# Row groups of four, reshuffles into 32 partitions, and a filter load over both halves in a fused FFT and MLP kernel

## The chip, the cores and the metric

The kernel runs on one core of one Trainium2 chip. The metric is device time in microseconds (us), smaller is better. Of the 25 runs of the kernel before that stood beside the three batches of experiments, 21 lie within 0.3% of their batch's median (357.52 to 362.08 us in all); a difference is called real here when it is over 2%, or when a 95% interval of the ratio excludes 1.

An engine name stands for the hardware unit in the profile: PE is TensorE, DVE is VectorE, ACT is ScalarE, POOL is GpSimd, and SP is SyncE, which here only issues transfers. "Hole" means a time in which TensorE had nothing in it. The granted clock is the share of its full speed at which TensorE was allowed to run.

## The reference

The kernel computes a forward pass and all its gradients (outputs 0 to 7). The part that matters here is the first block: a LayerNorm, a two-dimensional real FFT, a product with a learned complex filter, and the inverse FFT.

```python
def _A_ref(x, w_r, w_i):                      # x: 1 x 2048 x 448, w_r and w_i: 2048 x 225, bf16
    X = rfft2(x.astype(float32), axes=(-2, -1))
    W = w_r + 1j * w_i
    return irfft2(X * W, s=(S, D), axes=(-2, -1)).astype(bfloat16)

h  = x + _A_ref(layernorm(x), A_w_r, A_w_i)
h2 = h + _B_ref(layernorm(h), w1, b1, w2, b2)  # two-layer MLP with GELU over the sequence axis
# outputs: h2, then the gradients of x, w_r, w_i, w1, b1, w2, b2 for a given grad_out
```

## The kernel before

The FFT over 2048 rows is done as matmuls in two stages. In the first ("rows"), `row_a` transforms one of 16 row blocks and `row_b` transforms along the columns. The result has 128 partitions in one order; the second stage (`s2_stage`) wants 16 groups of 128 partitions in another. A DMA from SBUF to SBUF, called **reshuffle** below, puts it there. The tile `D2` is written by eight reshuffles of 226 KB in each direction:

```python
def row_b(h, quarters=False):
    u, c = divmod(h, 2)                       # a group is two rows
    ...                                       # four matmuls, then a cast into cs
    if c:
        defer(RESH_LAG, lambda: nc.sync.dma_start(out=D2[u:u + 121:8]..., in_=cs...), cs)
```

`D2[u:u + 121:8]` is 16 partitions at a stride of eight, over all 16 groups. While a reshuffle is under way, TensorE is kept busy with matmuls that do not depend on it ("fillers": `fill(20)` ahead of the forward second stage, `fill(N_FILL_B[2])` with 40 ahead of the backward one). Those that are not used up remain for the end of the kernel.

The filter, 2048 x 225 values of two bytes for each of its real and imaginary parts (921.6 KB a part), is loaded into `W_rows` and later copied by ScalarE and VectorE into a padded layout. The order of the partitions must match that of `D2`:

```python
def w_load():
    for c_, d in ((0, A_w_r), (1, A_w_i)):
        for p0, p1, j0, j1, row, dims in ((0, 64, 0, 16, 0, [[16 * DF, 4]]), (64, 112, 0, 16, 97, [[-16 * DF, 3]]),
                                          (112, 128, 0, 15, 113, []), (112, 128, 15, 16, 64, [])):
            nc.sync.dma_start(out=W_rows[p0:p1, c_, j0:j1, :],
                              in_=bass.AP(d.tensor, d.offset + row * DF,
                                          [[P * DF, 16]] + dims + [[1, (j1 - j0) * DF]]))
            yield
```

The list in square brackets is the access pattern of the source, slowest dimension first: `[stride, count]`. In every load of the kernel before, the slowest dimension of the source has a count of **16**. The loads of the real part are issued in the row loop at rows 9 to 12, those of the imaginary part at the start of the second stage, between two transposed blocks of w2 for the fillers (`"TWWWWTTT"`: T is a block of w2, W a filter load). All go through the queue of SyncE.

## Time and profile before

The kernel before takes 358.42 us (median of 3 runs, 358.37 to 358.54); its profiled run has a span of 357.2 us and a mean granted clock of 0.987. TensorE is busy in 341.5 us of it, so all that can be gained without removing matmuls is 15.7 us of holes. The table is made from the stage table that the prediction shows (a stretch less TensorE's busy time in it):

| Stretch | Holes, us | What ends the largest |
|---|---|---|
| start and forward rows, 0 to 31 | 6.86 | first loads; cast of a row on ScalarE, 1.61 |
| end of rows, 31 to 50.3 | 0.04 | |
| forward second stage, 50.3 to 105 | 2.94 | block of w2 from the DMA queue, 1.50; filter copies on ScalarE, 0.95 |
| middle, 105 to 236 | 0.15 | |
| backward rows, 236 to 254.5 | 0.70 | last LayerNorm rows on VectorE |
| backward second stage and inverse, 254.5 to 345 | 0 | |
| end, from 345 | 4.99 | cast, store and landing after the last matmul |

Two views of the transfers will be compared with the kernel after. The first is the table by stretches of four microseconds: start and end of the stretch, its length, busy time and count of PE, weight loads, DVE, ACT and POOL, then the granted clock, the share of the 16 DMA engines that was busy, and GB/s.

```profile
39.00:43.00 4.00, 3.96 (x37) 2.75 (x35) 3.20 (x8) 3.66 (x9) 0.00 (x0) 1.00 1.02 173
```

At 39 to 43 us the loads of the real filter part and the reshuffles run. The second view is the chain of waits, where one DMA stands in the whole second stage (start, duration, what):

```profile
52.00 8.60 DMA rO<-in_B_w_dram
```

That is the w2 block behind the imaginary filter part.

### The profile page before, as it was taken

How to read it: one execution, taken by the hardware profiler on the slowest of the kernel's cores; microseconds unless marked ns; L12 is line 12 of the kernel's file. 1: busy time of each engine (PE TensorE's matmuls, PEld its weight loads, DVE VectorE, ACT ScalarE, POOL GpSimd, SP SyncE). 2: the span in 40 equal slices, each digit the busy share in tenths (PEclk: the TensorE clock that was granted, in tenths of full speed). 3: DMA queues.
4: the chain of work that ended last, by engine and by line, in shares of the span. 5: the costliest groups of instructions: out<-in, count | busy, mean ns of one | idle time of the engine just before them, and what ended most of it. 6: DMA issues, size and time to landing. Idle time of an engine off the chain costs nothing.

```text
span 357.2 us, 6450 instructions
## 1 busy us (share of the span) xinstructions
PE 341.5 (96%) x2133; PEld 183.8 (51%) x2133; DVE 252.5 (71%) x679; ACT 213.8 (60%) x457; POOL 67.7 (19%) x227
## 2 busy tenths in 40 slices
PE   6898998899999999999999999999999999999994
PEld 2455665555645555555555555544444444455641
DVE  5897626992884888775226978784498766499994
ACT  4669836965986545504221355565477776588883
POOL 8667000000220000001001111110000000056771
PEclk9699999999999999999999999999999999999998
DMA  8999999847999999997886999999976878999996
GB/s 207 287 200 234 200 198 162 169 140 252 280 292 336 302 348 241 252 246 218 194 192 134 192 210 194 221 175 264 264 214 201 238 196 236 245 215 221 247 286 234
DMA packets 147672, 81.62 MB, mean 229 GB/s; under 512 B 95480, under 2 KB 139768, under 8 KB 147384
## 3 DMA queue, kind: packets, MB, share of 16 engines
q1 hardware_dynamic: 147352, 80.83, 94.7%
q8 instruction: 16, 0.26, 0.3%
q10 hardware_dynamic: 288, 0.39, 0.3%
q14 instruction: 16, 0.13, 0.1%
HBM read 27.56 MB, written 23.89 MB: 144 GB/s over the span
## 4 chain that ended last, share of the span: by engine, by line
PE 79%; ACT 7%; DVE 6%; DMA 4%; issue 2%; SPq 1%; POOL 0%; ACTq 0%; DVEq 0%
PE ps_mm L218 66%; PE ps_ff L218 13%; DMA rO<-in_B_w_dram 2%; ACT rO L82 2%; DVE stats L82 2%; ACT rG L82 1%; DMA rA<-in_A_x_dram 1%; DVE r L82 1%; ACT Ut L82 1%; DVE rA L82 1%; DVE rS L82 1%; SPq L297 1%; ACT Vt L82 1%; ACT rX L82 0%; ACT rS L82 0%
## 5 line engine op out<-in xcount | busy, mean ns | idle before, releaser
L218 PEld LDWEIGHTS <-r 128*128 128x128 bf16 (+2 forms) x660 | 61.7, 104 | 49.6 <-issue 2.7
L218 PEld LDWEIGHTS <-rS 128*128 128x128 bf16 (+2 forms) x496 | 40.5, 99 | 38.3 <-issue 7.0
L218 PE MATMUL ps_mm<-rD,r 128*128 128x448 bf16 x224 | 44.5, 352 | 0.0
L82 ACT CAST rO<-ps_mm 128x512 bf16<-128x512 f32 (+1 forms) x62 | 33.5, 583 | 13.8 <-PE ps_mm L218 11.1
L218 PE MATMUL ps_mm<-rC,rE 128*128 128x448 bf16 x144 | 36.0, 369 | 3.3 <-DMA rC<-in_grad_out_dram 3.3
L218 PEld LDWEIGHTS <-rst 128*128 128x128 bf16 (+1 forms) x320 | 23.8, 97 | 29.3 <-issue 13.5
L82 ACT CAST r<-ps_ff 128x452 bf16<-128x452 f32 x58 | 33.4, 576 | 8.8 <-PE ps_ff L218 8.4
L218 PE MATMUL ps_mm<-r,rst 128*128 128x512 bf16 (+3 forms) x192 | 36.4, 353 | 0.0
L218 PE MATMUL ps_mm<-rB,r 128*128 128x448 bf16 x160 | 31.2, 352 | 0.1
L218 PE MATMUL ps_mm<-rG,rst 128*128 128x512 bf16 (+1 forms) x128 | 28.2, 380 | 0.0
L82 ACT ACTIVATE r<-ps_mm,rstd_h 128x448 bf16<-128x448 f32 x16 | 10.1, 633 | 26.1 <-PE ps_mm L218 26.1
L82 ACT ACTIVATE r<-rC 128x448 bf16<-128x448 bf16 x16 | 9.1, 572 | 26.8 <-DMA out_dram<-r 12.9
L82 DVE SCALAR_TENSOR_TENSOR r<-ps_mm,b2col,r 128x448 bf16<-128x448 f32 x16 | 10.9, 682 | 19.9 <-PE ps_mm L218 17.9
L82 DVE CAST rO<-ps_mm 128x512 bf16<-128x512 f32 (+1 forms) x18 | 11.8, 658 | 15.2 <-PE ps_mm L218 14.3
L82 ACT ACTIVATE rG<-rG 128x896 bf16<-128x896 bf16 x14 | 13.3, 950 | 14.9 <-DVE rG L82 14.6
L218 PEld LDWEIGHTS <-rO 128*128 128x128 bf16 (+1 forms) x165 | 15.6, 98 | 12.2 <-DMA rO<-in_B_w_dram 1.8
L218 PE MATMUL ps_mm<-rE,rS 128*128 128x448 bf16 x112 | 21.5, 352 | 0.0
L82 ACT CAST rG<-ps_mm 128x512 bf16<-128x512 f32 (+1 forms) x33 | 16.6, 541 | 7.3 <-PE ps_mm L218 7.2
L1180 POOL TENSOR_SCALAR lcol<-lcol 128x1 f32<-128x1 f32 x16 | 8.5, 530 | 65.1 <-ACT r L82 65.1
L218 PE MATMUL ps_mm<-rC,rO 128*128 128x448 bf16 x80 | 19.1, 352 | 1.5 <-DMA rO<-in_B_w_dram 1.5
L1371 POOL TENSOR_SCALAR lcol<-lcol 128x1 f32<-128x1 f32 x16 | 5.5, 342 | 78.5 <-ACT r L82 78.5
L218 PEld LDWEIGHTS <-rE 128*128 128x128 bf16 x148 | 14.4, 101 | 11.3 <-issue 5.0
(198 smaller groups left out, 662.6 us busy)
## 6 DMA issues: line engine op xcount, KB each, us to landing
out_dram<-rO SPq DMA_DIRECT2D x34, 256.0 KB
r<-in_B_w_dram SPq DMA_DIRECT2D x5, 1024.0 KB
r<-r SPq DMA_DIRECT2D x16, 226.0 KB
r<-r SPq DMA_DIRECT2D x32, 113.0 KB
rS<-in_B_w_dram SPq DMA_DIRECT2D x4, 896.0 KB
out_dram<-rG SPq DMA_DIRECT2D x10, 256.0 KB
rO<-in_B_w_dram SPq DMA_DIRECT2D x2, 1024.0 KB
w_d<-rG SPq DMA_DIRECT2D x1, 1808.0 KB
```

The lines of the kernel that those rows point to most:

```text
L82: fn(**kw)
L218: nc.tensor.matmul(out, lhsT=lhsT, rhs=rhs, start=start, stop=stop)
L297: nc.sync.dma_start_transpose(out=wT, in_=B_w2[j * P:(j + 1) * P, :].rearrange("f (t c) -> f t c", c=P))
L1180: gp_.tensor_scalar(out=m1, in0=ms, scalar1=-1.0 / D, scalar2=None, op0=ALU.mult)
L1371: gp_.tensor_scalar(out=m1, in0=ms, scalar1=-2.0 / D, scalar2=None, op0=ALU.mult)
```

## The change

The intent: a group is four rows, so that a reshuffle covers 32 partitions at a stride of four and half of the second-stage groups, and the second stage's first groups need only the first halves. Each filter load then fills 32 partitions, every fourth over both halves of SBUF. As the transforms are grouped differently, they start later, the store of the filter gradient has 12 pieces, and fewer fillers stand ahead of the second stages. The core of the diff follows. The rest relabels generated constants to the new order, cuts the buffers for row groups from three to two (of twice the size) and those for folded rows from four to three, and adapts the backward rows and the store:

```diff
-N_FILL_B = (16, 16, 40, 8, 24, 8)
+N_FILL_B = (16, 16, 30, 8, 24, 8)
...
-            for p0, p1, j0, j1, row, dims in ((0, 64, 0, 16, 0, [[16 * DF, 4]]), (64, 112, 0, 16, 97, [[-16 * DF, 3]]),
-                                              (112, 128, 0, 15, 113, []), (112, 128, 15, 16, 64, [])):
-                nc.sync.dma_start(out=W_rows[p0:p1, c_, j0:j1, :],
+            for b, j0, j1, row, up in ((0, 0, 15, 0, 113), (0, 15, 16, 15, 49), (1, 0, 16, 16, 81), (2, 0, 16, 32, 49), (3, 0, 16, 48, 17)):
+                nc.sync.dma_start(out=W_rows[b:P:4, c_, j0:j1, :],
                                   in_=bass.AP(d.tensor, d.offset + row * DF,
-                                              [[P * DF, 16]] + dims + [[1, (j1 - j0) * DF]]))
+                                              [[up * DF, 2], [P * DF, 16], [1, (j1 - j0) * DF]]))
...
-            defer(RESH_LAG, lambda: nc.sync.dma_start(out=D2[u:u + 121:8].rearrange("p g c k -> p (g c k)"),
+            defer(RESH_LAG, lambda: nc.sync.dma_start(out=D2[u:u + 125:4, 8 * e:8 * e + 8].rearrange("p g c k -> p (g c k)"),
...
-        row_b(t - 1)
+        row_b(t - 3)
         if t == NT - 1:
-            row_b(t)
+            for i in range(t - 2, NT):
+                row_b(i)
...
-        for _ in range((9, 10, 11, 12).count(t)):
+        for _ in range((9, 9, 10, 11, 12).count(t)):
             next(w_loads)
...
-    fill(20)
+    fill(14)
...
-            for kind in "TWWWWTTT":
+            for kind in "TWWWWWTTT":
...
-    GW_AT = (1, 3, 5, 6, 7, 9, 11, 12)
+    GW_AT = (1, 2, 3, 4, 5, 6, 7, 8, 9, 10, 11, 12)
```

More of the change, by code (lines that the diff above doesn't have):

```diff
@@ L356 @@
     fr = ftmp(448, 64)
-    gp_.iota(fr.rearrange("p (c i g) -> p c i g", c=2, i=4), pattern=[[1, 2], [16, 4], [2, 8]], base=0,
+    gp_.iota(fr.rearrange("p (c q i g) -> p c q i g", c=2, q=2, i=4), pattern=[[1, 2], [8, 2], [16, 4], [2, 4]], base=0,
              channel_multiplier=0, allow_small_or_imprecise_dtypes=True)
@@ L432, in gen_R @@
         t = ftmp(2688, P).bitcast(I32)
-        tv = t.rearrange("p (c h x) -> p c h x", c=2, h=2)
-        f2 = fr.rearrange("p (c x) -> p c x", c=2)
+        tv = t.rearrange("p (c h x) -> p c h x", c=4, h=2)
+        f2 = fr.rearrange("p (c x) -> p c x", c=4)
         for h in range(2):
@@ L443, in decode @@
         a4, fc, s_, c_, f_ = col(), col(), col(), col(), col()
-        floor_div(eng, a4, pcolb, 64)
-        gp_madd(s_, a4, -64.0, pcolb)
-        floor_div(eng, fc, s_, 8)
-        gp_madd(s_, fc, -8.0, s_)
-        gp_madd(s_, s_, 2.0, a4)
+        floor_div(eng, a4, pcolb, 32)
+        gp_madd(s_, a4, -32.0, pcolb)
+        floor_div(eng, fc, s_, 4)
+        gp_madd(s_, fc, -4.0, s_)
+        gp_madd(s_, s_, 4.0, a4)
         floor_div(eng, c_, fc, 4)
@@ L501, in gen_UV @@
             d0 = dst[:, :, 0:64].rearrange("p g (l f) -> p g l f", f=4)
-            d1 = dst[:, :, 64:112].rearrange("p g (l f) -> p g l f", f=3)
+            d1 = dst[:, :, 64:P].rearrange("p g (l f) -> p g l f", f=4)
             for j in range(4):
                 m = msk[:, j:j + 1]
-                dj = d1[:, :, :, j - 1] if j else dst[:, :, 112:128]
-                for o, c in ((d0[:, :, :, j], 0), (dj, 1)):
+                for o, c in ((d0[:, :, :, j], 0), (d1[:, :, :, j], 1)):
                     if load[1] + 0.24 < load[0] + 0.38:
@@ L564, in w_io @@
         for c_, d in ((0, dr), (1, di)):
-            for p0, p1, g0, g1, row, dims in ((0, 64, 0, 16, 0, [[16 * DF, 4], [1, 16 * DF]]),
-                                              (64, 112, 0, 16, 112, [[-DF, 48], [1, DF]]),
-                                              (112, 128, 1, 16, 127, [[-DF, 15], [1, DF]]),
-                                              (112, 128, 0, 1, 64, [[1, DF]])):
-                sb = Wv[p0:p1, g0:g1, c_, 0:DF]
+            for sl, g0, g1, row, dims in ((slice(0, 64), 0, 16, 0, [[16 * DF, 4], [1, 16 * DF]]),
+                                          (slice(65, P, 4), 0, 16, 112, [[-DF, 16], [1, DF]]),
+                                          (slice(66, P, 4), 0, 16, 96, [[-DF, 16], [1, DF]]),
+                                          (slice(67, P, 4), 0, 16, 80, [[-DF, 16], [1, DF]]),
+                                          (slice(64, P, 4), 1, 16, 127, [[-DF, 15], [1, DF]]),
+                                          (slice(64, P, 4), 0, 1, 64, [[1, DF]])):
+                sb = Wv[sl, g0:g1, c_, 0:DF]
                 d_ap = bass.AP(d.tensor, d.offset + row * DF, [[P * DF, 16]] + dims)
@@ L615, in rowbase @@
         return 32 * (s_ // 4) + s_ % 4
-    blk_ring = ring(rS, 0, 3, 8, 2, P // 2)
-    fold_ring = ring(rS, 6 * 4 * P, 4, 912)
+    blk_ring = ring(rS, 0, 2, 8, 2, 4, P // 4)
+    fold_ring = ring(rS, 8 * 4 * P, 3, 912)
     blks, css = {}, {}
@@ L665, in row_a @@
             mm(pa[:, k * P:(k + 1) * P], lhsT=ft[:, o:o + P], rhs=R, start=True, stop=True)
-        if t % 2 == 0:
-            blks[t // 2] = blk_ring.next()
-        evac(out=blks[t // 2][:, :, t % 2, :], in_=pa[:].rearrange("p (a b) -> p a b", a=8))
+        if t % 4 == 0:
+            blks[t // 4] = blk_ring.next()
+        evac(out=blks[t // 4][:, :, :, t % 4, :], in_=pa[:].rearrange("p (a e b) -> p a e b", a=8, e=2))
     def row_b(h, quarters=False):
-        u, c = divmod(h, 2)
-        if u < 0 or u >= NT // 2:
+        u, e, c = h // 4, h // 2 % 2, h % 2
+        if h < 0 or h >= NT:
             return
@@ L679, in row_b @@
                 if quarters:
-                    mm(pq[:, 1 - w, b, :], lhsT=blks[u][0:DC, 2 * (2 * w + b) + c].rearrange('p j x -> p (j x)'),
+                    mm(pq[:, 1 - w, b, :], lhsT=blks[u][0:DC, 2 * (2 * w + b) + c, e].rearrange('p j x -> p (j x)'),
                        rhs=csB[0:DC, w, b, 0:KW // 2], start=True, stop=True)
                     continue
-                mm(pv[:, 1 - w, :], lhsT=blks[u][0:DC, 2 * (2 * w + b) + c].rearrange('p j x -> p (j x)'), rhs=csF[0:DC, w, b, :],
+                mm(pv[:, 1 - w, :], lhsT=blks[u][0:DC, 2 * (2 * w + b) + c, e].rearrange('p j x -> p (j x)'), rhs=csF[0:DC, w, b, :],
                    start=(b == 0), stop=(b == 1))
         if c == 0:
-            css[u] = cs_ring.next()
-        cs = css[u]
+            css[h // 2] = cs_ring.next()
+        cs = css[h // 2]
         if quarters:
@@ L900 @@
     for c in range(2):
-        sc.copy(out=Rp.rearrange("p (a q b c) -> p c a q b", c=2, q=8, a=4)[:, c],
-                in_=Rm[:, 64 * c:64 * c + 64].rearrange("p (q a b) -> p a q b", q=8, a=4))
+        for e in range(2):
+            sc.copy(out=Rp.rearrange("p (e a q b c) -> p c e a q b", e=2, c=2, q=8, a=2)[:, c, e],
+                    in_=Rm[:, 64 * c + 32 * e:64 * c + 32 * e + 32].rearrange("p (q a b) -> p a q b", q=8, a=2))
     FILL_A = (3, 3, 3, 3, 3, 3, 3, 3, 3, 3, 3, 3, 3, 3, 3, 3)
@@ L1242, in rows @@
             row_a(t, Rm[:])
-        fill(2)
-        row_b(t - 2, True)
-        fill(2)
+            fill(2)
+        row_b(t - 4, True)
+        fill(2 if t < NT else 1)
     for t in range(NT):
@@ L1337 @@
     load_W(3)
-    for t in range(NT - LAG, NT + 2):
+    for t in range(NT - LAG, NT + 4):
         if t == 13:
```

## The prediction

> **What bounds the kernel now.** I read the page first for the share of each engine, then a table of busy time by stage, then the chain of waits and the engines' own timelines around the holes. The page:
>
> ```profile
> span 357.2 us, 6450 instructions
> PE 341.5 (96%) x2133; PEld 183.8 (51%) x2133; DVE 252.5 (71%) x679; ACT 213.8 (60%) x457; POOL 67.7 (19%) x227
> ```
>
> TensorE has something in it for all but 15.7 us of the span. Each of its 2133 matmuls is there again after the change (the listing of both kernels' instructions gives 2133 in each, with the same shapes). So only the holes can shrink, or new ones open. The stage table (columns: span of the stretch, then busy us and instructions of PE, weight loads, DVE, ACT, POOL; granted clock; DMA share; GB/s) says where they are:
>
> ```profile
> 0.00:25.00 25.00, 19.76 (x99) 9.93 (x100) 19.47 (x83) 13.20 (x26) 17.16 (x86) 0.86 0.99 237
> 25.00:31.00 6.00, 4.38 (x35) 2.75 (x33) 5.88 (x22) 5.51 (x12) 4.59 (x18) 1.00 1.01 213
> 31.00:50.30 19.30, 19.26 (x153) 12.81 (x152) 10.09 (x28) 12.84 (x26) 3.90 (x18) 1.00 1.01 194
> 50.30:70.00 19.70, 17.20 (x124) 10.84 (x122) 13.87 (x35) 15.17 (x31) 0.11 (x1) 1.00 1.08 195
> ...
> 236.00:254.50 18.50, 17.80 (x118) 7.69 (x116) 10.52 (x22) 10.24 (x19) 0.64 (x1) 1.00 0.98 231
> 254.50:300.00 45.50, 45.50 (x261) 21.68 (x259) 34.17 (x71) 33.57 (x67) 0.00 (x0) 1.00 0.80 219
> 300.00:345.00 45.00, 45.00 (x327) 24.81 (x324) 35.21 (x103) 34.41 (x88) 21.80 (x57) 1.00 0.99 236
> 345.00:357.20 12.20, 7.21 (x44) 3.03 (x42) 7.26 (x22) 4.74 (x11) 3.54 (x8) 0.89 0.72 271
> ```
>
> Holes, span less PE: 5.2 us in the start, 1.6 at 25 to 31 (forward rows), 2.5 at 50 to 70 (forward second stage), 0.7 at 236 to 254 (backward rows), none in the backward second stage and inverse rows, 5.0 after the last matmul; the stretches not shown hold 0.6. The causes of the ones the change can touch, from the PE timeline:
>
> ```profile
> 30.04 0.56 PE L218 MATMUL ps_ff<-csF,rS 112*128 112x226 bf16 x4 [1.61 <-ACT rS L82]
> 60.65 0.55 PE L218 MATMUL ps_mm<-rC,rO 128*128 128x448 bf16 x2 [1.50 <-DMA rO<-in_B_w_dram]
> 68.63 0.35 PE L218 MATMUL ps_ff<-r,Vt 128*128 128x452 bf16 x1 [0.95 <-ACT rX L82]
> 240.34 0.40 PE L218 MATMUL ps_ff<-Rm,rS 128*128 128x128 bf16 x4 [0.70 <-DVE rS L82]
> ```
>
> The first waits for the cast of a row that stands behind three generator instructions on ScalarE; the second for a transposed block of w2 from the DMA queue; the third for ScalarE, which copies the filter into its padded layout between casts; the fourth for the last LayerNorm rows. No wait for a reshuffle (the copy into the second stage's 16 x 128 layout) is on the path. The queue's own timeline shows that the late w2 block is queued behind reshuffles and filter loads:
>
> ```profile
> 41.59 5.57 SPq L693 DMA_DIRECT2D r<-r  x3
> 47.25 2.24 SPq L297 DMA_TRANSPOSE rO<-in_B_w_dram  x1
> 49.55 2.35 SPq L583 DMA_DIRECT2D rB<-in_A_w_i_dram  x4
> 52.00 5.02 SPq L297 DMA_TRANSPOSE rO<-in_B_w_dram  x1
> ```
>
> [...] the chain of waits has 14 such matmuls in 2.65 us, 189 ns each. [...]
>
> **The change, part by part.**
>
> *Four rows to a group.* Column transforms now start when four rows are in, not two. In the forward loop the transform of row t-1 becomes that of row t-3, so four transforms stand after the last row instead of two. Counts do not change: 16 casts per direction, 16 reshuffles of 226 KB. By row 7 (the 1.61 us hole) two casts of 0.54 us have not yet been asked of ScalarE and VectorE, up to 1.1 us less in front of the late cast. But TensorE has two transforms less by then too, 8 matmuls at about 0.095 us, 0.8 us, and where VectorE paces the rows (4.96 of 5.00 us busy at 20 to 25) that turns into idling. Net about -0.3.
>
> *Reshuffle by halves.* The two reshuffles of a group fill second-stage groups 0 to 7 and 8 to 15. The first second-stage matmul waits now only for the first-half copies; in the listing of waits it holds four DMA semaphores instead of five, and the rest move to group 8. The last first-half copy is released after transform 13, two transforms (0.8 us) before the end of the rows. That pays for the cut of the filler ahead of the stage: 20 to 14 w2 matmuls, 6 x 0.19 = 1.1 us. From the last needed transform to the stage's first use: before 23 fillers x 0.19 + 0.2 = 4.6 us; after 17 x 0.19 + 0.2 + 0.8 = 4.2 us. No wait was seen at 4.6, and issue to last landing took at most 3.1 us there (issues end at 47.2, use at 50.3), so I expect 0, at worst 0.5. Backward: before 42 filler steps, 9.7 us by the PE timeline (244.86 to 254.56, 48 matmuls, 0.23 us a step); after, two transforms (0.4 us) and 33 steps, 8.0 us: 0. Moved fillers are the same matmuls run later and cost nothing in themselves.
>
> *The w2 wait at 59.2 to 60.65.* The cut filler puts six w2 matmuls behind two more second-stage groups of 0.38 us: TensorE asks for the block 0.8 us later relative to its work. The imaginary filter part, 922 KB, is written before it in the queue[...]. One more load per part costs the queue about 0.6 us of issue. So the block arrives perhaps 1 us sooner and is wanted 0.8 us later: the 1.5 us goes. Against it stands the third hole. The listing gives ScalarE 7 of the 16 filter copies, before 5; one takes 0.95 us there and 0.41 on VectorE, so ScalarE gets 1.9 us more in a stretch where it already held TensorE up. Also each copy reads all partitions' loads now and waits for all five of a part. I give back 0.7. Net -0.8.
>
> *Filter store in 12 pieces, not 8.* Same bytes, four more issues of about 0.6 to 0.8 us on a queue that does not bound the end: 0.
>
> *Backward fillers.* Before, 68 steps run ahead of the backward second stage (20 in the rows, 8 ahead of row 14, 40 in the gap), after it 54 (16, 8 and 30). So 54 steps instead of 40 are left for the end: the last run of 46 matmuls (chain of waits, from 344.4) becomes one of about 62. VectorE's last gradient rows, which end at 351.4 beside the last matmuls, get 14 x 0.23 = 3.2 us more cover, and the stores of the last pieces find a less loaded queue. The tail of 5.0 us is cast, store and landing and stays, with perhaps -0.3. The 0.7 at 240.3 stays: fillers between rows 13 and 14 are as before.
>
> Sum: -0.3 + 0 - 0.8 + 0 - 0.3 = -1.4, so 357.0 from 358.4. The fillers look retuned for this layout, which makes a miscount in the bad direction less likely, so I lean to 356.7.
>
> **Rivals.** (1) Both forward holes and the third vanish (1.6 + 1.5 + 0.95 = 4.0) and the tail gives 0.5: 353.9. For it: every one of them hangs on queues that get shorter. Against: ScalarE is 5.51 of 6.00 and 4.90 of 5.00 us busy in two of the three. (2) A reshuffle takes the place: with shorter filler the copy lands after the first second-stage matmul wants it, forward 0.5 to 1.5 us, with DMA share at 1.0; 358 to 359. Against it the 4.2 us just worked out. (3) ScalarE becomes the bound at 57 to 70 with two slow copies more, and what the w2 wait gives is lost whole: 358. (4) VectorE paces the first rows and the deferred transforms only add behind: +0.8 us, 358.
>
> **Range and chances.** All holes that the change can reach sum to about 5 us, 1.4%, and new waits of more than 2 us have no visible cause. The 8-in-10 range is 354.2 to 358.9. Faster by over 2% needs 351.2, more than all reachable holes: 0.03. Slower by over 2% needs 365.6: 0.02. Within: 0.95.
>
> **What would show it.** Right: PE busy stays near 341; the wait on the w2 block is gone or under 0.5 us; no PE wait for a DMA at the start of either second stage; the wait for ScalarE's filter copies is as large as before or larger; the wait on row 7's cast is shorter; at the end the last run of weight-gradient matmuls is about 16 longer and the tail about 5 us. Wrong: a PE wait for a reshuffle, a PE sum that differs by over 2 us, or holes in the backward half, where I expect none but the 0.7.

## The result, and the profile after

The changed kernel is correct and takes **381.58 us** (median of 3 runs, 380.56 to 382.19). Ratios in this document are the mean time of one kernel's fast runs over that of the other's in the same rounds, so they are not quite the ratio of the medians. Here it is 1.0642 (95% interval 1.0605 to 1.0678): 6.4% slower, and far outside the predicted range. The page of the changed kernel, its first lines and its chain of waits by engine:

```profile
span 378.5 us, 6454 instructions
PE 343.5 (91%) x2133; PEld 184.8 (49%) x2133; DVE 255.0 (67%) x680; ACT 214.5 (57%) x457; POOL 70.0 (18%) x227
...
PE 76%; DMA 10%; DVE 6%; ACT 5%; issue 2%; SPq 1%; POOL 0%; DVEq 0%; ACTq 0%
```

TensorE does the same 2133 matmuls in 343.5 us, 2.0 more than before. The span is 21.3 us longer. So 19.3 us are new holes. Transfers hold 10% of the chain; before it was 4%. TensorE's timeline says where. Its columns are start, duration, the instruction, and in brackets the idle time ahead of it and what ended it:

```profile
30.37 0.56 PE L218 MATMUL ps_ff<-csF,rS 112*128 112x226 bf16 x4 [1.79 <-ACT rS L82]
58.57 0.53 PE L218 MATMUL ps_ff<-r,Vt 128*128 128x452 bf16 x1 [7.73 <-DMA r<-r]
83.52 0.93 PE L218 MATMUL ps_mm<-rC,rO 128*128 128x448 bf16 x2 [12.59 <-DMA rO<-in_B_w_dram]
```

The second line is the first matmul of the second stage, which waits 7.73 us for a reshuffle; there was no such wait. The third is the w2 wait, which was 1.50 us and is 12.59. Together they are 18.8 of the 19.3 us. The start adds 2.0 (holes to 31 us: 8.86 against 6.86, by the stage table of this kernel); the filter-copy wait of 0.95 is gone in this kernel, and the tail is 0.94 shorter (4.05 against 4.99). The added busy time goes with the clock: two matmuls after the long wait take 0.93 us, where the same two took 0.55 before, and the granted clock stood at 0.50 there.

Neither of the two waits is for the filter itself. They are for transfers that stand behind it in the queue. SyncE's own timeline (start, time until the issues were through, what, count) shows the order:

```profile
34.74 1.82 SPq L583 DMA_DIRECT2D rB<-in_A_w_r_dram  x3
37.56 1.06 SPq L583 DMA_DIRECT2D rB<-in_A_w_r_dram  x2
...
42.31 7.24 SPq L693 DMA_DIRECT2D r<-r  x4
49.64 9.22 SPq L297 DMA_TRANSPOSE rO<-in_B_w_dram  x1
58.92 2.90 SPq L583 DMA_DIRECT2D rB<-in_A_w_i_dram  x5
61.91 18.06 SPq L297 DMA_TRANSPOSE rO<-in_B_w_dram  x1
```

The five loads of a part go out in about 3 us. The transfers after them are held: one w2 block takes 9.22 us to issue and the next 18.06, where the same block after the imaginary part took 5.02 before. The chain of waits gives the two transfers from issue to use:

```profile
47.35 11.09 DMA r<-r
...
61.91 21.55 DMA rO<-in_B_w_dram
```

The w2 block needs 21.55 us, against 8.60 before. And the table by stretches of four microseconds says what the DMA engines did meanwhile:

```profile
39.00:43.00 4.00, 3.71 (x32) 2.48 (x31) 2.91 (x8) 4.00 (x9) 0.00 (x0) 1.00 0.13 50
...
63.00:67.00 4.00, 4.00 (x33) 2.66 (x31) 2.96 (x10) 3.47 (x11) 0.11 (x1) 1.00 4.45 81
...
71.00:75.00 4.00, 0.00 (x0) 0.00 (x0) 0.00 (x0) 0.00 (x0) 0.00 (x0) 1.00 0.12 52
75.00:79.00 4.00, 0.00 (x0) 0.00 (x0) 0.00 (x0) 0.00 (x0) 0.00 (x0) 0.65 0.13 54
```

No compute engine has anything to do from 71 to 79 us, and the DMA share is 0.12 to 0.13, which is **two engines of 16**, moving 52 to 54 GB/s, 26 to 27 an engine. This is not a queue that is full; it is a queue in which two engines work off something large and 14 stand idle. 921.6 KB at 52 GB/s take 17.7 us. A share cannot be read this way everywhere: from 63 to 67 us it is 4.45 at only 81 GB/s, because a packet counts from its start to its end, and 18 packets of 256 bytes that started there stayed open for about 15 us each. VectorE's first copy out of the imaginary part starts at 80.35 us, 18.5 us after the last of its loads was issued at 61.82.

What is new in the loads is their access pattern. The old ones lead with 16 rows of the source; the new ones lead with `[up * DF, 2]`, the two halves. That this leading count sets the number of engines, 16 before and two now, is a guess up to here, and the prediction did not ask about it. A second guess goes with it: a reshuffle over 16 engines queued behind the filter has two of its sixteen shares waiting behind it, and is not complete before they are. That would explain why other transfers are late, and the experiments test both.

The kept traces also record the start and end of every packet and the completions that the engines post; a transfer counts here as landed with its last completion. The views only sum these records up, but they show the two engines and the waiting shares directly. A filter load posts 16 completions in the kernel before and two in the changed one; its packets of 7200 bytes are in flight 16 at a time before and two at a time after (medians). From first to last packet a part takes 6.4 us (real) and 5.3 us (imaginary) before, 19.8 and 19.3 after. Of each of the first three reshuffles issued behind the real part, 14 of 16 completions had come by 49.77 us; the last two came between 56.18 and 58.44 us, and the matmul that waits starts at 58.57. The real part's last packet had ended at 56.21.

### The profile page after: what moved, and what is told of

Its sections match the earlier page's. It is cut to its first block, busy times and chain, and to the rows that moved or that the text cites. A ratio compares the mean times of both kernels' runs of the same rounds, so it can differ in the third digit from the quotient of the medians.

```text
span 378.5 us, 6454 instructions
## 1 busy us (share of the span) xinstructions
PE 343.5 (91%) x2133; PEld 184.8 (49%) x2133; DVE 255.0 (67%) x680; ACT 214.5 (57%) x457; POOL 70.0 (18%) x227
## 4 chain that ended last, share of the span: by engine, by line
PE 76%; DMA 10%; DVE 6%; ACT 5%; issue 2%; SPq 1%; POOL 0%; DVEq 0%; ACTq 0%
PE ps_mm L218 63%; PE ps_ff L218 13%; DMA rO<-in_B_w_dram 6%; DMA r<-r 3%; ACT rO L82 2%; DVE stats L82 2%; DVE r L82 1%; DMA rA<-in_A_x_dram 1%; ACT Ut L82 1%; SPq L297 1%; DVE rA L82 1%; DVE rS L82 1%; ACT Vt L82 1%; ACT rS L82 0%; DVE mvx L82 0%
## 5 line engine op out<-in xcount | busy, mean ns | idle before, releaser
L218 PEld LDWEIGHTS <-r 128*128 128x128 bf16 (+1 forms) x660 | 62.0, 104 | 50.1 <-issue 3.4
L82 ACT CAST rO<-ps_mm 128x512 bf16<-128x512 f32 (+1 forms) x66 | 35.2, 579 | 11.3 <-PE ps_mm L218 10.8
L218 PE MATMUL ps_mm<-rC,rE 128*128 128x448 bf16 x144 | 37.3, 380 | 3.6 <-DMA rC<-in_grad_out_dram 2.6
L218 PEld LDWEIGHTS <-rst 128*128 128x128 bf16 (+1 forms) x320 | 23.8, 97 | 29.0 <-issue 13.8
L82 ACT CAST r<-ps_ff 128x452 bf16<-128x452 f32 x56 | 31.7, 574 | 8.3 <-PE ps_ff L218 7.1
L218 PE MATMUL ps_mm<-rC,rO 128*128 128x448 bf16 x80 | 20.0, 366 | 12.6 <-DMA rO<-in_B_w_dram 12.6
L1182 POOL TENSOR_SCALAR lcol<-lcol 128x1 f32<-128x1 f32 x16 | 8.5, 530 | 64.7 <-ACT r L82 64.7
L218 PE MATMUL ps_ff<-csI,rAT 113*128 113x224 bf16 (+1 forms) x108 | 19.0, 297 | 0.6 <-ACT rAT L82 0.4
L218 PE MATMUL ps_ff<-r,Vt 128*128 128x452 bf16 x32 | 12.2, 380 | 7.8 <-DMA r<-r 7.7
L82 ACT CAST rG<-ps_mm 128x512 bf16<-128x512 f32 (+1 forms) x28 | 14.4, 550 | 8.1 <-PE ps_mm L218 8.0
```

The lines of the kernel that those rows point to most:

```text
L82: fn(**kw)
L218: nc.tensor.matmul(out, lhsT=lhsT, rhs=rhs, start=start, stop=stop)
L1182: gp_.tensor_scalar(out=m1, in0=ms, scalar1=-1.0 / D, scalar2=None, op0=ALU.mult)
```

## The experiments

Theory A: the leading dimension of 2 puts each filter load on two engines, and that alone costs what was lost. Rival B: writes into 32 partitions at a stride of four are slow in themselves. Rival C: the cut fillers and the later transforms leave too little cover. Twelve kernels were run in three batches. The kernel before, run beside each batch on the same chip, had medians of 359.15, 359.0 and 358.99 us.

### 1. The same loads, split into their two halves

```diff
-                nc.sync.dma_start(out=W_rows[b:P:4, c_, j0:j1, :],
-                                  in_=bass.AP(d.tensor, d.offset + row * DF,
-                                              [[up * DF, 2], [P * DF, 16], [1, (j1 - j0) * DF]]))
+                for hf in range(2):
+                    nc.sync.dma_start(out=W_rows[64 * hf + b:64 * hf + 64:4, c_, j0:j1, :],
+                                      in_=bass.AP(d.tensor, d.offset + (row + up * hf) * DF,
+                                                  [[P * DF, 16], [1, (j1 - j0) * DF]]))
```

Ten loads a part in place of five; same bytes, same partitions at a stride of four, same fillers and transforms. The leading dimension is 16, and each load covers 16 partitions of one half in place of 32 of both (experiments 3 and 4 leave the partitions alone).

> The changed kernel with each of the ten filter loads (32 partitions, DRAM pattern with a leading dimension of 2) issued as its two halves, 16 partitions each at stride 4 with a leading dimension of 16; same bytes to the same places, everything else as changed. Theory A (the leading dimension of 2 puts each load on two of the 16 DMA engines; the changed kernel shows a DMA share of 0.12 to 0.13 and 52 to 54 GB/s while it waits): the plateau is gone, the wait of 7.7 us for the reshuffle falls under 1 us, that of 12.6 us for the w2 block falls to 0 to 4 us (ten more issues of 0.6 us stand before it), time 357 to 363 us. Rival B (writes to 32 partitions at stride 4 are slow in themselves, filter or reshuffle): stays over 375. Rival C (the filler cut from 20 to 14 matmuls no longer covers the reshuffles): the 7.7 us wait stays, time about 366 to 370.

Measured: correct, 359.81 us (358.11 to 360.5), ratio to before 1.0008 (0.9967 to 1.0048). TensorE's timeline has no wait for a reshuffle any more, and one for w2:

```profile
64.71 0.55 PE L218 MATMUL ps_mm<-rC,rO 128*128 128x448 bf16 x2 [2.05 <-DMA rO<-in_B_w_dram]
```

So 22 us go with the leading dimension and nothing else of the change. Rivals B and C keep their cause in this kernel and lose their effect. The 2.05 us that remain have twice the number of loads ahead of them: SyncE spends 6.27 us issuing ten, against 2.35 for the four of before.

### 2. Only the imaginary part split

The same edit under a condition: the real part keeps the leading 2.

> As split_halves for the imaginary part alone; the real part is still loaded with a leading dimension of 2. Theory A with one part for each wait: the wait for the reshuffle at the start of the second stage stays at 6 to 9 us (the real part is in front of it), the wait for the w2 block falls to 0 to 4 us; time 366 to 371 us. Rival B or C: the w2 wait stays about 12 us, time 378 to 384.

Measured: correct, 369.77 us (one look, state unknown). The reshuffle wait stays, a little longer than the 6 to 9 us I had written, and the w2 wait is gone:

```profile
60.30 0.53 PE L218 MATMUL ps_ff<-r,Vt 128*128 128x452 bf16 x1 [9.66 <-DMA r<-r]
```

So the real part, issued in the row loop, makes the reshuffle late, and the imaginary part makes the w2 block late. Each wait belongs to the part that is queued ahead of it.

### 3. and 4. The kernel before, with a leading dimension of 2, and of 4

In the kernel before nothing is changed but the source pattern of its four loads a part. Bytes, partitions, fillers and transforms are those of before. The rows are wrong. The stride of the leading dimension is one row short of contiguous, so that the pattern cannot be written as one dimension.

```diff
-                                              [[P * DF, 16]] + dims + [[1, (j1 - j0) * DF]]))
+                                              [[8 * P * DF - DF, 2], [step * DF, (p1 - p0) // 2], [1, (j1 - j0) * DF]]))
```

For the second kernel it is `[4 * P * DF - DF, 4]` and a quarter of the partitions.

> The kernel before, nothing of the change in it, with only the DRAM side of its own four filter loads per part written with a leading dimension of 2 that does not merge (it reads partly other rows: the result is wrong on purpose; bytes, destinations and number of transfers as before). Theory A: slower by 12 to 24 us, a DMA share near 0.125 and about 53 GB/s while TensorE waits. Rivals B and C: as before, within 1 us of 358.4.

> As before_lead2 with a leading dimension of 4 (wrong on purpose too). Theory A says four engines: a plateau at a DMA share of 0.25 and about 107 GB/s if it shows at all, the 17 us of a part's load become 8 to 9, slower than before by 2 to 10 us, clearly less than before_lead2. If the leading dimension only matters as 'not the 16 of before' (no proportion), the same as before_lead2.

Measured: with 2, 392.63 us (389.77 to 392.99), ratio 1.092 (1.0872 to 1.0968); with 4, 372.07 us (one look). Both results are wrong. The kernel with 2, its waits and a stretch of its table:

```profile
63.88 0.54 PE L218 MATMUL ps_ff<-r,Vt 128*128 128x452 bf16 x1 [14.31 <-DMA r<-r]
90.02 0.93 PE L218 MATMUL ps_mm<-rC,rO 128*128 128x448 bf16 x2 [15.09 <-DMA rO<-in_B_w_dram]
...
75.00:79.00 4.00, 0.00 (x0) 0.00 (x0) 0.39 (x1) 0.75 (x2) 0.00 (x0) 1.00 0.13 52
```

The same of the kernel with 4 (one run, state unknown):

```profile
54.35 0.54 PE L218 MATMUL ps_ff<-r,Vt 128*128 128x452 bf16 x1 [4.41 <-DMA r<-r]
71.53 0.93 PE L218 MATMUL ps_mm<-rC,rO 128*128 128x448 bf16 x2 [6.16 <-DMA rO<-in_B_w_dram]
...
63.00:67.00 4.00, 2.37 (x18) 1.30 (x15) 2.33 (x8) 2.27 (x5) 0.00 (x0) 1.00 0.26 96
```

A leading 2 gives a share of 0.13 and 52 GB/s, a leading 4 gives 0.26 and 96 GB/s, so 26 and 24 GB/s an engine. The time follows: 16 engines 359, four 372, two 393. The completions agree: a filter load posts four with a leading 4 and two with a leading 2, and reshuffles behind them complete in 12 and 4, or 14 and 2. Theory A stands, with a dose. Both kernels lost more than I expected (33 us against 12 to 24, and 13 against 2 to 10). The kernel before has more to lose than the changed one, 33 against 23. In part its loads took longer: 23.8 us (real) and 21.1 us (imaginary) from first to last packet, against 19.8 and 19.3. Whether its form of the reshuffle adds to that (experiments 9 and 10) was not tested.

### 5. Loads that all lead with 16, and no more of them than needed

The changed kernel again. The lower half of SBUF holds consecutive rows and can be loaded in one transfer of 64 partitions; the upper half takes five. All lead with 16 at the source, and with 16 or 64 partitions at the destination. Six loads a part.

```diff
-            for b, j0, j1, row, up in ((0, 0, 15, 0, 113), (0, 15, 16, 15, 49), (1, 0, 16, 16, 81), (2, 0, 16, 32, 49), (3, 0, 16, 48, 17)):
-                nc.sync.dma_start(out=W_rows[b:P:4, c_, j0:j1, :],
+            for sl, j0, j1, row, dims in ((slice(0, 64), 0, 16, 0, [[16 * DF, 4]]), (slice(64, P, 4), 0, 15, 113, []),
+                                          (slice(64, P, 4), 15, 16, 64, []), (slice(65, P, 4), 0, 16, 97, []),
+                                          (slice(66, P, 4), 0, 16, 81, []), (slice(67, P, 4), 0, 16, 65, [])):
+                nc.sync.dma_start(out=W_rows[sl, c_, j0:j1, :],
...
-                                              [[up * DF, 2], [P * DF, 16], [1, (j1 - j0) * DF]]))
+                                              [[P * DF, 16]] + dims + [[1, (j1 - j0) * DF]]))
```

The counts of loads in the row loop become `(9, 9, 10, 10, 11, 12)`, and the list at the second stage `"TWWWWWWTTT"`.

> The changed kernel with its filter loads written as six per part, every one with 16 as its leading dimension on both sides (the lower half in one load of 64 partitions, the upper in sets of 16). Theory A (only the leading dimension of 2 cost the 23 us; the rest of the change is worth about what was predicted): no wait for a reshuffle at the second stage, the w2 wait between 0.5 and 2.0 us, start hole 7.0 us and tail about 3.5 us as in the run with split loads; 357.5 to 360. Rival B (writes at a stride of four partitions are slow in themselves): the upper half is still at stride four, so a reshuffle or w2 wait of over 4 us stays and the time is over 364.

Measured: correct, **356.6 us** (356.47 to 357.31, 6 runs), ratio to before 0.9928 (0.9899 to 0.9957). That is faster than both kernels, by 0.7% and by 25 us. The stage table of this run:

```profile
0.00:25.00 25.00, 18.69 (x91) 8.71 (x92) 19.52 (x82) 12.61 (x26) 17.75 (x86) 0.86 1.00 237
25.00:31.00 6.00, 4.16 (x32) 2.54 (x31) 5.87 (x22) 5.51 (x11) 4.59 (x18) 1.00 1.18 196
...
50.30:70.00 19.70, 18.76 (x134) 11.87 (x133) 15.99 (x39) 16.71 (x33) 0.82 (x3) 1.00 0.99 187
...
345.00:357.00 12.00, 6.97 (x43) 3.01 (x42) 4.97 (x13) 3.87 (x8) 1.65 (x3) 0.88 0.48 179
```

Its span is 355.5 us, 1.7 less than before. Worked out as for the table of before: holes to 31 us 8.15 (before 6.86), in the forward second stage to 70 us 0.94 (2.50), at the end 10.5 - 6.97 = 3.53 (4.99). The w2 wait is gone, where I had expected 0.5 to 2.0 us, and the time lies 0.9 us below what I expected.

### 6. All twelve loads in the row loop

```diff
-        for _ in range((9, 9, 10, 10, 11, 12).count(t)):
+        for _ in range((7, 7, 8, 8, 9, 9, 10, 10, 11, 11, 12, 12).count(t)):
...
-            for kind in "TWWWWWWTTT":
+            for kind in "TTTT":
```

> The same, with all twelve filter loads issued in the row loop, so none stands between two blocks of w2 in the queue. If the wait for the w2 block comes only from the filter loads queued ahead of it, it goes (under 0.3 us) and the time is 1.0 to 2.0 us under the run before, 356 to 358. Rival: the early loads share the 16 DMA engines with the reshuffles, and a wait for a reshuffle of 0.5 us or more at the second stage takes the place; then the time is 358 to 361.

Measured: correct, 357.4 us (356.88 to 358.56), ratio 0.9948 (0.9918 to 0.9978), span 355.2. No wait for w2 and none for a reshuffle. It is in the expected range of time, but not faster than the run before: there was no w2 wait left to remove.

### 7. The kernel before, with its loads in the row loop

```diff
-        for _ in range((9, 10, 11, 12).count(t)):
+        for _ in range((8, 8, 9, 9, 10, 10, 11, 12).count(t)):
...
-            for kind in "TWWWWTTT":
+            for kind in "TTTT":
```

> The kernel before with nothing changed but the place of its filter loads: all eight issued in the row loop, none between two blocks of w2. Tests the step of the prediction that put a price of 1.5 us on the w2 wait. If that wait is on the path as read, it goes and the time falls by 1.0 to 1.5 us, to about 357. Rival: the time stays within 0.5 us because a wait for a reshuffle (under 1.5 us) opens at the second stage, or because ScalarE's filter copies take up the gain (its wait of 0.95 us grows to over 1.8).

Measured: correct, 364.74 us (362.79 to 365.7), ratio 1.0134 (1.0094 to 1.0173). A miss for both expectations: the w2 wait does go, but a reshuffle wait opens that is more than three times as long as I had allowed.

```profile
55.76 0.54 PE L218 MATMUL ps_ff<-r,Vt 128*128 128x452 bf16 x1 [5.27 <-DMA r<-r]
```

The changed kernel with the same early loads had none (experiment 6). So something in the change makes the reshuffles less tight.

### 8. The kernel before, with the fillers moved to the end

`N_FILL_B[2]` is 26 in place of 40, nothing else.

> The kernel before with 26 in place of 40 filler steps ahead of the backward second stage, so that 54 steps are left for the end as in the changed kernel. Tests the step that gave the longer last run of matmuls only 0.3 us. If the tail falls from 5.0 to about 3.5 us, as it did in the run with split loads, the fillers alone do it: 357 to 357.7. Rival (the tail there came from the store in 12 pieces): the tail stays at 4.7 to 5.0 and the time within 0.5 us of before. A wait for a reshuffle at the backward second stage would show as a hole near 250 us; none is expected, as 28 fillers, over 6 us, still stand ahead of it.

Measured: correct, 360.02 us (359.37 to 362.12), ratio 1.0025 (0.9991 to 1.0058). The tail does fall, from 4.99 to 4.0 us. But the backward second stage now waits:

```profile
252.81 0.35 PE L218 MATMUL ps_ff<-r,Vt 128*128 128x452 bf16 x1 [2.10 <-DMA r<-r]
```

The wait had been expected not to be there, at over 6 us of cover. Moving the fillers gains 1.0 us and costs 2.1. This run also gives a measure of the noise: its forward half is that of the kernel before, and its w2 wait is 1.07 us in place of 1.50.

### 9. and 10. The new form of the reshuffle in the kernel before

Both earlier edits together (loads in the row loop, 26 fillers), and each of the eight reshuffles writes 32 partitions and half of the groups. The data land in wrong places; the result is wrong. In the second kernel the two halves are exchanged, so that the last reshuffle fills the groups that the second stage wants first.

```diff
-            defer(RESH_LAG, lambda: nc.sync.dma_start(out=D2[u:u + 121:8].rearrange("p g c k -> p (g c k)"),
+            defer(RESH_LAG, lambda: nc.sync.dma_start(out=D2[u // 2:u // 2 + 125:4, 8 * (u % 2):8 * (u % 2) + 8].rearrange("p g c k -> p (g c k)"),
```

In the second, `8 * (1 - u % 2)` in place of `8 * (u % 2)`.

> The kernel before with its eight filter loads all in the row loop and 26 filler steps ahead of the backward second stage, as in the two runs before (waits for a reshuffle of 5.27 us forward and 2.10 us backward), and with one more edit: each reshuffle writes 32 partitions at a stride of four and one half of the second-stage groups, as the changed kernel does (rows land in wrong places on purpose: the result is wrong). If the new form of the reshuffle is what lets the changed kernel's good versions go without these waits, both waits fall below 0.5 us, and the time is 356 to 358. If it is the form of the filter loads or the order of transforms, the waits stay at 4 to 6 and 1.5 to 2.5 us, and the time is 364 to 368.

> The same with the two halves of the groups exchanged, so that the very last reshuffle fills groups 0 to 7, which the second stage wants first (wrong on purpose too). It tells the number of partitions written from the order. If the width of 32 partitions makes each copy land sooner, the waits stay below 1 us forward and backward. If it is only that the first groups no longer wait for the last copy, the waits come back, to over 2 us forward and over 1 us backward.

Measured: the first 356.61 us (356.42 to 357.72), ratio 0.9948 (0.9918 to 0.9978); the second 359.2 us (358.01 to 360.13), ratio 1.0015 (0.9974 to 1.0056). The first has this forward wait, and none of 0.4 us or more at the backward second stage:

```profile
50.73 0.36 PE L218 MATMUL ps_ff<-r,Vt 128*128 128x452 bf16 x1 [0.98 <-DMA r<-r]
```

The second, with the halves exchanged, has these two (the view could name no releaser for the first; by the completions the last reshuffle landed at 51.72 us):

```profile
51.81 0.35 PE L218 MATMUL ps_ff<-r,Vt 128*128 128x452 bf16 x1 [1.93 <-issue]
251.97 0.36 PE L218 MATMUL ps_ff<-r,Vt 128*128 128x452 bf16 x1 [0.54 <-DMA r<-r]
```

Set against experiments 7 and 8, which have one of the two edits each (the two together with the old form were not run), the new form takes the forward wait from 5.27 to 0.98 us and the backward one from 2.10 to under 0.4. It is not down to zero forward, as I had written, but it is most of it. With the order against it, 1.93 and 0.54 remain: so about 3.3 of the 4.3 us forward, and 1.6 of at least 1.7 backward, come from the form (32 partitions and half of the groups), and the rest from the order. The completions agree: from its first packet to its landing, the last backward reshuffle takes 1.60 us in experiment 8 and 1.61 in the kernel before, 1.15 and 1.12 us in these two. The traces of experiments 9 to 12 lack 7 of the 2133 matmul records each, so their sums are uncertain by some tenths. What in the form does it, the number of partitions or their places, these two runs do not separate.

### 11. The kernel before, with the transforms of row t-3

```diff
-        row_b(t - 1)
+        row_b(t - 3)
         if t == NT - 1:
-            row_b(t)
+            for i in range(t - 2, NT):
+                row_b(i)
```

> The kernel before with only the order of forward transforms changed: that of row t-3 in place of t-1 at each row, four after the last row, as in the changed kernel. Tests rival 4 of the prediction (VectorE paces the first rows and deferred transforms only add behind). If it holds, the start hole grows from 5.2 to between 6.2 and 7.2 us and the wait on row 7's cast stays at 1.6 to 1.8; the time rises by 1 to 2 us, more if a reshuffle now comes late at the second stage. If the prediction's step holds, the holes up to 31 us sum to 6.8 or less (before 6.8), and the time stays within 0.5 us.

Measured: correct, 361.08 us (360.74 to 361.34), ratio 1.0066 (1.0039 to 1.0093). The start, from the stage table:

```profile
0.00:25.00 25.00, 17.80 (x94) 8.72 (x95) 19.89 (x84) 12.71 (x24) 17.93 (x87) 0.93 0.99 237
25.00:31.00 6.00, 6.00 (x50) 4.04 (x49) 5.96 (x22) 5.63 (x11) 4.60 (x18) 1.00 1.15 179
```

The holes to 31 us sum to 7.20: the first stretch loses 2.0 us (7.20 against 5.24), as rival 4 has it, and the wait on the late cast disappears, as the prediction's step has it and better. The net of 0.34 us is within the noise: the traces of the kernel before and of the six other kernels here with the same code for the first rows have 6.86 to 7.87. So no effect of the later transforms on the start is shown. The larger part of the 2.1 us that this kernel loses is later: a reshuffle wait of 1.04 us, and a w2 wait of 2.01 in place of 1.50.

### 12. Still more fillers for the end

Experiment 5 with `N_FILL_B[2]` at 20 in place of 30.

> The changed kernel with loads led by 16, and 20 in place of 30 filler steps ahead of the backward second stage, so that ten more are left for the end. If the filler covers the tail further, it falls from 3.5 to about 2.5 us and the time to about 355.6. Rival: a reshuffle comes late at the backward second stage (8.0 us of cover become 5.7, and the kernel before had a wait of 2.10 us at about 6.5), a hole near 250 us of 0.5 us or more, and the time is 356.5 to 358; or the tail is at its floor, and the time stays the same.

Measured: correct, 359.73 us (358.93 to 360.34), ratio 1.0027 (0.9997 to 1.0057). The backward second stage now waits:

```profile
250.53 0.35 PE L218 MATMUL ps_ff<-r,Vt 128*128 128x452 bf16 x1 [1.63 <-DMA r<-r]
```

The tail is no shorter either: the last matmul ends at 354.4 and the span at 358.2. So 20 is too few here; more than 30 was not tried.

## Why the prediction was wrong

**The reading of before was right.** The holes, and what each waited for, were read correctly, and the two transfers that mattered were named, the reshuffle and the w2 block behind the filter. The error was in what the change does to the queue they share.

**The step that failed** is "*The w2 wait at 59.2 to 60.65*", in the words "So the block arrives perhaps 1 us sooner". It took the rate of a load from the partitions it writes, an assumption of mine that no trace of this case showed. What changed was the number of DMA engines, and the leading dimension of 2 gave two (two completions a load, a DMA share of 0.12 to 0.13). A part takes 19.3 to 19.8 us from first to last packet, against 5.3 to 6.4 before; the w2 block was not 1 us sooner but, by the chain, 13 us slower from issue to use (21.55 against 8.60). Shown by experiments 1 and 2, which remove the waits with the leading dimension, by 3 and 4, which make them in the kernel before, and by the completions. The term was -0.8 and was +11.1 (12.59 less 1.50), before the 0.95 us of the filter-copy wait.

**Reshuffle by halves, "0, at worst 0.5".** It was +7.73 forward, by the same cause through the real part, which is queued ahead of the last reshuffles (experiment 2). The step counted the cover of 4.2 us correctly (0.19 us for a w2 matmul: 23 in 4.35 us in the chain of waits of before) and never asked what stands in front of the reshuffle. With loads on 16 engines (experiment 5) the wait is 0, as worked out, and backward, where no filter load is ahead, it was 0 in the changed kernel too. What the step missed on the good side: the new form makes the copies land sooner (the last backward one 1.12 to 1.15 us after its first packet, in place of 1.60), and only that lets fillers be moved away (experiments 7 to 10). The 4.6 us of cover in the kernel before held next to no slack: the last reshuffle landed at 50.01 us, and the matmul that needs it started at 50.31. With all filter loads ahead the same reshuffle was 5.27 us late.

**What it gives back.** The 0.7 us for ScalarE's copies was not needed: with the loads right the filter-copy wait is 0.91 us, against 0.95. So once the load is repaired this stretch gives 1.56 us (2.50 less 0.94), against 0.8.

**Row groups, -0.3.** In experiment 5 the holes to 31 us are 1.3 us larger, and the wait on the cast of row 7 is longer (1.79), not shorter. The loss is more than noise: six traces with the new start have 7.93 to 9.06 us, seven with the old one 6.86 to 7.87. Rival 4 had the sign right, but the later transforms that it blamed show no effect of their own (experiment 11). What makes it is not settled; candidates that no run separates are the fewer buffers for folded rows (three for four), the two more ScalarE copies ahead of the row loop and the changed casts of the rows.

**Fillers and tail, -0.3.** The last run of matmuls in the chain of waits is 59 long in the changed kernel and in experiment 5 and 62 in experiment 1, about as predicted (46 before). The direction was right, the term is mis-sized: in experiment 5 the tail is 1.46 us shorter. Moving the fillers alone gives 1.0 (experiment 8). The rest may be the store in 12 pieces, which was not tried by itself. In the changed kernel the tail is 0.94 us shorter.

**TensorE near 341 us.** It was 343.5. The granted clock fell in and after the two long waits (0.50 from 58.57 to 62 us, 0.65 from 75 to 79, 0.53 from 79 to 87), and the matmuls right after them were longer (two took 0.93 us in place of 0.55).

**The sum.** With the load repaired the holes change by +1.3 (start), +0.3 (end of rows), -1.6 (w2 and copies), +0.2 (to 105 us) and -1.5 (tail), -1.3 in all; TensorE's busy time adds -0.4, and the span falls by 1.7. The prediction of 356.7 is near what the change gives when its loads use 16 engines: 356.6. That it is so near is in part luck: the start was off by 1.6 us in one direction, the w2 stretch and the tail by 0.8 and 1.2 in the other. The one omitted term is 25 us. **The chances** said that "new waits of more than 2 us have no visible cause". It was visible, in the diff: the leading count of the access pattern goes from 16 to 2. Rival 2 named the reshuffle wait, at 0.5 to 1.5 us, from the cut filler; none of the four asked how fast the changed transfers are.

## What to carry to other kernels

Whenever a DMA's access pattern is rewritten, look at its slowest dimension first: here that of the source set how many of the 16 engines worked (two with a leading 2, four with 4, 16 with 16), and with a leading 2 a filter part took 19.3 to 23.8 us from first to last packet in place of 5.3 to 6.4, in experiment 3 with the same partitions and bytes. Here it was enough to split the transfers so that 16 leads (experiments 1 and 5: no wait for a reshuffle, and 2.05 us and none for w2). A slow transfer is paid for by what is queued behind it (7.73 us of wait for a reshuffle and 12.59 for a w2 block), so look in the trace for waits on other transfers and for stretches with a low rate and a DMA share near 2/16 or 4/16 (0.12 to 0.13 at 52 to 54 GB/s and 0.26 at 96 here). And judge a change with several parts only after the broken part is repaired: here the rest was worth 0.7%, and its useful core, the new form of the reshuffle, was worth something because it let other work move.
